# Stage 2's scores as products over 64 rows with two experts side by side, q and k kept unstacked, and three buffers of transposed probabilities

## The chip, the core and the metric

The program runs on one core of one Trainium2 chip. The metric is the device time of one execution in microseconds (us). TensorE multiplies, VectorE (DVE), ScalarE (ACT) and GpSimd (POOL) work on its operands and results, and SyncE (SP) issues the DMAs in one queue.

## The reference, cut to what matters

Eight batches of 576 rows pass through three stages. Stage 1 is an attention over 32 memory slots per head (8 heads of 64), the MLP mixes and applies a 512 to 2048 to 512 network, and stage 2 is a layer of four attention experts with 64 columns each, of which two are chosen for every row:

```python
# stage 1, per batch and head
a = softmax(phi)                       # over s, eps in the sum
k_m, v_m = a.T @ k, a.T @ v            # 32 x 64
attn = softmax(q @ k_m.T / 8) @ v_m
# mlp, per batch
u = x + (U @ V mixing over the sequence)
x = u + relu(u @ w_ch1) @ w_ch2
# stage 2, per batch
logits = x @ w_gate; top 2 of 4, weights w by softmax
for e in range(4):
    q, k, v = x @ wq[e], x @ wk[e], x @ wv[e]        # 576 x 64
    scores = q @ k.T / 8, causal
    ye = softmax(scores) @ v @ wo[e]
    out += (w of e where e was chosen) * ye
```

Every matrix product is made of three float16 products: both operands are split into a high and a low half, and high by high, high by low and low by high are added up in PSUM.

## The kernel before, in words

The batches are pipelined: in the loop over b (1 to 6) the MLP of batch b, stage 2 of batch b-1 and stage 1 of batch b+1 are put into one list of generator steps, ordered by a due time. One unit of due time is one item of the MLP, and a batch has 64 items of 12 matmuls each (`up`, L1000, and `down`, L1016). The last MLP and the last two stages 2 (called P and L in the list) follow `ORDER2`, a list written out by hand of which step comes when. A scheduler then sets each engine's order from the steps, their dependencies and the free buffers.

Stage 2 of a batch: `proj` (L1103) makes q and k of an expert pair `ep` (two experts, 2 x 64 lanes) for half the sequence, 288 columns. Its result is evicted into stacked tiles: `qst` holds for each expert the high half of q on lanes 0 to 63 and the low half on lanes 64 to 127; `khs` holds the high half of k twice, `kls` the low half twice. For q that takes two ACT copies (L1118) and two DVE subtractions (L1121) on 64 lanes, for k two ACT copies (L1125), two DVE subtractions (L1128), two more ACT copies (L1131) and one DVE copy (L1133).

`unit_s(i, ep, eo)` makes the scores of row block i (0 to 3) for one expert eo of the pair: two matmuls over 128 rows, (i+1)*128 columns wide (L1223, L1224), into one PSUM bank. Both split products of the high k and the low one are made at once by the stacking. Then come mask and maximum (DVE, L1227), exponential and high half (ACT, L1233, L1234), low half (POOL, L1236), and a transposing DMA into `pT` (SP, L1238), of which there are two buffers. `unit_s_last` does the last 64 rows of both experts in one go: eight matmuls of 64 weight columns and 288 columns (L1251, L1252), where one expert's result lies on PSUM lanes 0 to 63 and the other's on 64 to 127. `unit_v` (L1300) multiplies `pT` with v; its due time stands `A_LAG` = 4.2 units after that of its `unit_s`. `unit_o` and `unit_w` follow it.

In stage 1, `pair_scores` (L685 to L687) multiplies q with the memory keys: for each of six blocks of 96 rows three matmuls, whose weights have 96 columns, 64 columns wide.

PSUM has four banks called "a" that stage 1, `proj`, `vg`, the scores and small sums share, three "m" for the MLP, and one "v" for `unit_v`.

Of the kernel before, what the change touches and what calls it, by code (L numbers as in the profile page):

```python
# [20 lines left out]
P = 128  # L21
# [20 lines left out]
PRB, OBB = 1, 1  # L42


B_GAP, A_GAP, A_LAG = 10, 2.2, 4.2

START, SLACK, SLACK2, LATER = 53, 1.5, 4, 2

# [102 lines left out]
def kernel(ctx: ExitStack, tc: tile.TileContext, q, k, v, phi, U, V, w1, w2, wg, wq, wk, wv, wo, out):  # L151
# [27 lines left out]
    def ps_a(name):  # L179
        return ps.tile([P, 512], F32, tag="a", bufs=4, name=name)  # L180
# [326 lines left out]
    def stage1(b):  # L507
# [101 lines left out]
        def pair_scale(p):  # L609
            s = bpool.tile([P, 3], F32, tag="ps", bufs=4, name="ps")  # L610
            r = bpool.tile([P, 3], F32, tag="pi", bufs=2, name="pi")
            t = bpool.tile([P, 2], F32, tag="pt", bufs=6, name="pt")
            sb["s", p] = t
            sb["sc", p] = s
            yield from scales(largest(sb.pop(("arr", p))), s, r, down=2.0 ** -13)
            yield 0.1
            dve.scalar_tensor_tensor(t[:, 0:1], r[:, 2:3], 1.0 / 32.0, r[:, 0:1], op0=ALU.mult, op1=ALU.mult)
            dve.tensor_scalar(t[:, 1:2], r[:, 1:2], 1.0 / 64.0, None, op0=ALU.mult)
# [60 lines left out]
        def pair_scores(p):  # L679
            kb, vb = sb.pop(("kb", p))  # L680
            qT = sb.pop(("qT", p))
            psc = ps_a(f"ss{b}_{p}")
            for c in range(C):
                o = psc[:SP, c * 64:(c + 1) * 64]
                pe.matmul(o, qT[:, 0, c], kb[:, 0], start=True, stop=False)  # L685
                pe.matmul(o, qT[:, 0, c], kb[:, 1], start=False, stop=False)
                pe.matmul(o, qT[:, 1, c], kb[:, 0], start=False, stop=True)  # L687
            sb["psc", p] = psc
            pv = ps_a(f"vt{b}_{p}")
            pe.transpose(pv[:, 0:P], vb, ident)  # L690
            hf, pp = divmod(p, 2)
            if pp == 0:
                sb["vtf", hf] = bpool.tile([P, 2, P], F32, tag="vtf", bufs=1, name="vtf")
                sb["vth", hf] = bpool.tile([P, 2, 2, P], F16, tag="vth", bufs=2, name="vth")
            vtf, vth = sb["vtf", hf], sb["vth", hf]
            yield 0.4
            act.activation(vtf[:, pp], pv[:, 0:P], AF.Copy)
            act.activation(vth[:, pp, 0], pv[:, 0:P], AF.Copy)
            yield 0.4
            pool.tensor_tensor(vth[:, pp, 1], vtf[:, pp], vth[:, pp, 0], op=ALU.subtract)  # L700
# [13 lines left out]

        def half_kb_first(hf):
            pk = sb.pop(("pk", hf))
            iv = bpool.tile([P, 3], F32, tag="iv", bufs=2, name="iv")
            dve.tensor_scalar(iv[:, 2:3], pk[:, P:P + 1], EPS, None, op0=ALU.add)
            yield 0.1
            dve.reciprocal(iv[:, 2:3], iv[:, 2:3])  # L720
# [320 lines left out]
    def stage2(b):  # L1041
# [11 lines left out]
        def room(v, o, n):  # L1053
            return v[:, o:o + n]
# [40 lines left out]
        def proj(which, ep, h_):  # L1095
            yhl = s2["yhl"]
            w = (wqs, wks)[which]
            pp = ps_a(f"pj{b}_{which}_{ep}_{h_}")
            n = 0
            ts_ = slice(h_ * NH, (h_ + 1) * NH)  # L1100
            for kc in range(KC):
                for a, c in ((0, 0), (0, 1), (1, 0)):
                    pe.matmul(pp[:, 0:NH], w[:, a, kc, ep * P:(ep + 1) * P], yhl[:, c, kc, ts_],  # L1103
                              start=(n == 0), stop=(n == 3 * KC - 1))
                    n += 1
            yield 0.7
            if h_ == 0:
                for j, nm in enumerate((("qst",), ("khs", "kls"))[which]):
                    if tail:
                        o = 2 * KC * S + 2 * NT * NE * D + (3 * ep + which + j) * 2 * S  # L1110
                        s2[nm, ep] = room(v1, o, 2 * S).rearrange("p (e s) -> p e s", e=2)
                    else:
                        s2[nm, ep] = ap.tile([P, 2, S], F16, tag=nm, name=nm)
            src = [pp[eo * 64:eo * 64 + 64, 0:NH] for eo in range(2)]
            if which == 0:
                qst = s2["qst", ep]
                for eo in range(2):
                    act.activation(qst[0:64, eo, ts_], src[eo], AF.Copy)  # L1118
                yield
                for eo in range(2):  # L1120
                    dve.tensor_tensor(qst[64:128, eo, ts_], src[eo], qst[0:64, eo, ts_], op=ALU.subtract)  # L1121
            else:
                khs, kls = s2["khs", ep], s2["kls", ep]
                for eo in range(2):
                    act.activation(khs[0:64, eo, ts_], src[eo], AF.Copy)  # L1125
                yield
                for eo in range(2):
                    dve.tensor_tensor(kls[0:64, eo, ts_], src[eo], khs[0:64, eo, ts_], op=ALU.subtract)  # L1128
                yield
                for eo in range(2):  # L1130
                    act.activation(khs[64:128, eo, ts_], src[eo], AF.Copy)  # L1131
                yield
                dve.tensor_copy(kls[64:128, :, ts_], kls[0:64, :, ts_])  # L1133

        def vg(i):
            n = P if i < NT - 1 else TAIL
# [69 lines left out]
        def p_tiles(nb, k):  # L1206
            if tail:
                pr = ring(k, v2, 0, 2 * S, 3).bitcast(F32)
                phl = ring(k, v2, 6 * S, 2 * NT * P, 4)
                pT = ring(k, v2, 6 * S + 8 * NT * P, 2 * NT * P, 6)[:, 0:nb * P].rearrange("p (n q) -> p n q", q=P)  # L1210
                return pr, phl, pT
            pr = ap.tile([P, S], F32, tag="pr", bufs=PRB, name="pr")
            phl = ap.tile([P, 2 * NT * P], F16, tag="phl", bufs=2, name="phl")
            pT = ap.tile([P, nb, P], F16, tag="pT", bufs=2, name="pT")
            return pr, phl, pT

        def unit_s(i, ep, eo):
            qst, khs, kls = s2["qst", ep], s2["khs", ep], s2["kls", ep]
            cs = s2["ysc"][3]
            n = (i + 1) * P  # L1220
            nb = 2 * (i + 1)
            psc = ps_a(f"sc{b}_{i}_{ep}_{eo}")
            pe.matmul(psc[:, 0:n], qst[:, eo, i * P:n], khs[:, eo, 0:n], start=True, stop=False)  # L1223
            pe.matmul(psc[:, 0:n], qst[:, eo, i * P:n], kls[:, eo, 0:n], start=False, stop=True)  # L1224
            yield 0.5
            nm = ap.tile([P, 1], F32, tag="nm", bufs=4, name="nm")
            dve.tensor_tensor_reduce(psc[:, 0:n], psc[:, 0:n], wmask[:, (NT - 2 - i) * P:(NT - 1) * P], cs, 3.0e38, ALU.add, ALU.min, nm)  # L1227
# [12 lines left out]

        def unit_s_last(ep):
            i = NT - 1
            qst, khs, kls = s2["qst", ep], s2["khs", ep], s2["kls", ep]
            cs = s2["ysc"][3]
            psc = [ps_a(f"sc{b}_{i}_{ep}_{h_}") for h_ in range(2)]
            nb = 2 * NT
            N = NT * P
            for h_ in range(2):
                for eo in range(2):
                    o = psc[h_][eo * 64:eo * 64 + TAIL, 0:NH]  # L1250
                    pe.matmul(o, qst[:, eo, i * P:S], khs[:, eo, h_ * NH:(h_ + 1) * NH], start=True, stop=False)  # L1251
                    pe.matmul(o, qst[:, eo, i * P:S], kls[:, eo, h_ * NH:(h_ + 1) * NH], start=False, stop=True)  # L1252
            yield
            nm = ap.tile([P, 4], F32, tag="nml", bufs=2, name="nml")
            for h_ in range(2):
# [303 lines left out]
```

## Time and profile before

| | |
|---|---|
| median of 3 runs | 1362.08 us (1360.62 to 1370.35) |
| profiled execution, its own time | 1368.24 us |
| span of the profiled execution | 1366.3 us |
| PE busy | 1242.5 us (91%) |
| DVE busy | 938.0 us (69%) |
| ACT busy | 786.8 us (58%) |
| POOL busy | 409.2 us (30%) |

The profile lists for each engine its instructions with start and duration, and for each idle stretch what ended it. A matmul's duration runs from its start to the end of its result, while the next matmul starts long before; what a matmul costs an engine that is never idle is the distance from its start to the start of the next one. The timeline gives these starts; it merges like instructions that follow each other and gives their number.

### The profile page before, as it was taken

The numbers are of one execution on the slowest core, as the hardware profiler recorded it, in microseconds if no ns is written. First come the engines' busy times: TensorE is split into PE (matmuls) and PEld (weight loads), VectorE is DVE, ScalarE is ACT, GpSimd is POOL, SyncE is SP. The second block draws the span as 40 slices with busy tenths as digits, with TensorE's granted clock in tenths as the row PEclk, the third lists the DMA queues.
The fourth block names the chain that finished last, engine by engine and source line by source line (L and its number), as shares of the span: only waits on it lengthen the run. The fifth ranks groups of instructions, "written<-read, shape, count | busy, mean of one in ns | idle before, by whom it ended". The sixth has DMA issues, their size and how long they took to land. (4 is left out here: it accounts for less than half of the span.)

```text
span 1366.3 us, 31204 instructions
## 1 busy us (share of the span) xinstructions
PE 1242.5 (91%) x11932; PEld 950.9 (70%) x11932; DVE 938.0 (69%) x2791; ACT 786.8 (58%) x1886; POOL 409.2 (30%) x379
## 2 busy tenths in 40 slices
PE   5657897999999999999999999999999999999997
PEld 4435675777767777777777777677877777787764
DVE  7899777876577656876667766676667765554464
ACT  3885653665565654665655565565556566433476
POOL 3556620242322332332322323333222323001121
PEclk9778898999999999999999999999999999999999
DMA  9744141054412433244322434235232323102235
GB/s 253 229 141 123 36 89 27 21 97 73 89 48 61 92 75 60 58 83 89 74 60 61 85 59 87 58 74 98 57 69 63 75 57 63 49 14 41 39 77 113
DMA packets 257158, 106.42 MB, mean 78 GB/s; under 512 B 203792, under 2 KB 248528, under 8 KB 257008
## 3 DMA queue, kind: packets, MB, share of 16 engines
q1 hardware_dynamic: 257008, 104.43, 34.4%
q8 instruction: 93, 1.52, 0.5%
q14 instruction: 57, 0.47, 0.1%
HBM read 52.21 MB, written 9.44 MB: 45 GB/s over the span
## 5 line engine op out<-in xcount | busy, mean ns | idle before, releaser
L1000 PE MATMUL up<-uhl,w1s 128*128 128x288 f16 x3072 | 428.6, 293 | 27.2 <-DVE h L1006 22.5
L1016 PE MATMUL dn<-h,w2s 128*128 128x288 f16 x3072 | 411.8, 287 | 4.6 <-DVE u L1023 2.4
L1000 PEld LDWEIGHTS <-w1s 128*128 128x128 f16 x3072 | 301.3, 100 | 119.1 <-issue 34.9
L1016 PEld LDWEIGHTS <-w2s 128*128 128x128 f16 x3072 | 295.2, 98 | 84.4 <-issue 8.5
L1236 POOL TENSOR_TENSOR phl<-pr,phl 128x128 f16<-128x128 f32 (+3 forms) x112 | 92.5, 826 | 338.8 <-ACT phl L1234 253.1
L1006 DVE SCALAR_TENSOR_TENSOR h<-up,h 128x288 f16<-128x288 f32 x256 | 113.5, 451 | 60.5 <-ACT h L1004 59.3
L1004 ACT ACTIVATE h<-up 128x288 f16<-128x288 f32 x256 | 101.1, 402 | 85.3 <-PE up L1000 83.2
L605 DVE TENSOR_REDUCE amax<-raw 96x1 f32<-96x768 f32 x72 | 68.1, 946 | 87.2 <-DMA raw<-in_v_dram 46.5
L638 POOL TENSOR_TENSOR kvq<-raw,kvq 96x768 f16<-96x768 f32 x48 | 78.3, 1650 | 134.8 <-ACT raw L632 134.8
L1233 ACT ACTIVATE pr<-sc,nm 128x128 f32<-128x128 f32 (+3 forms) x112 | 58.8, 525 | 103.9 <-DVE nm L1227 54.1
L1023 DVE SCALAR_TENSOR_TENSOR u<-dn,us,u 128x288 f32<-128x288 f32 x128 | 65.2, 511 | 45.1 <-PE dn L1016 44.3
L1300 PEld LDWEIGHTS <-pT 128*128 128x128 f16 (+1 forms) x1260 | 56.5, 102 | 36.4 <-DMA pT<-phl 19.0
L1300 PE MATMUL av<-vhl,pT 128*128 128x64 f16 (+1 forms) x1260 | 68.7, 195 | 14.2 <-DMA pT<-phl 12.6
L1227 DVE CUSTOM_DVE_ANT_0 sc<-sc,wmask,ysc 128x128 f32<-128x128 f32 (+3 forms) x128 | 69.6, 549 | 9.3 <-PE sc L1224 8.1
L626 ACT ACTIVATE kvq<-raw,ps 96x768 f16<-96x768 f32 x72 | 63.0, 924 | 9.2 <-DVE ps L265 9.1
L1234 ACT ACTIVATE phl<-pr 128x128 f16<-128x128 f32 (+3 forms) x112 | 52.3, 467 | 15.3 <-DMA pT<-phl 13.2
L1337 ACT ACTIVATE ohl<-av,fac 128x64 f16<-128x64 f32 (+1 forms) x140 | 35.7, 307 | 41.9 <-DVE fac L1313 21.7
L1358 PE MATMUL wo<-wos,oT 128*128 128x512 f16 (+1 forms) x288 | 57.5, 351 | 2.5 <-DMA oT<-ohl 1.3
L1103 PE MATMUL pj<-yhl,wqs 128*128 128x288 f16 x336 | 47.6, 290 | 5.6 <-ACT u L885 4.9
L1103 PEld LDWEIGHTS <-wqs 128*128 128x128 f16 x384 | 38.0, 101 | 17.8 <-issue 6.8
L1151 PE MATMUL vg<-wvg,yhl 128*128 128x260 f16 (+1 forms) x504 | 48.5, 256 | 0.0
L1103 PE MATMUL pj<-yhl,wks 128*128 128x288 f16 x336 | 46.3, 286 | 0.0
(323 smaller groups left out, 2264.7 us busy)
## 6 DMA issues: line engine op xcount, KB each, us to landing
w1s<-in_moe_w_ch_dram SPq DMA_DIRECT2D x32, 256.0 KB, 5.1
w2r<-in_moe_w_ch_dram SPq DMA_DIRECT2D x8, 1024.0 KB, 5.1
out_dram<-ob SPq DMA_DIRECT2D x28, 256.0 KB, 2.2
raw<-in_k_dram SPq DMA_DIRECT2D x48, 144.0 KB, 2.6
raw<-in_v_dram SPq DMA_DIRECT2D x48, 144.0 KB, 2.9
raw<-in_q_dram SPq DMA_DIRECT2D x48, 144.0 KB, 2.5
phi<-in_phi_dram SPq DMA_DIRECT2D x16, 288.0 KB, 3.8
rx<-in_k_dram SPq DMA_DIRECT2D x16, 144.0 KB, 4.6
```

The lines of the kernel that those rows point to most:

```text
L605: dve.tensor_reduce(o, raw, axis=AX.XYZ, op=ALU.max, apply_absolute_value=True)
L626: act.activation(hl[:, 0], src, AF.Copy, scale=s[0:SP, j:j + 1])
L638: pool.tensor_tensor(hl[:, 1], src, hl[:, 0], op=ALU.subtract)
L1000: pe.matmul(pm, w1s[:, f // 2, a, kc, f % 2 * P:f % 2 * P + P], uhl[c][:, kc], start=(n == 0), stop=(n == 3 * KC - 1))
L1004: act.activation(hb[:, 0, g], pm, AF.Relu)
L1006: dve.scalar_tensor_tensor(hb[:, 1, g], pm, 0.0, hb[:, 0, g], op0=ALU.max, op1=ALU.subtract)
L1016: pe.matmul(pm, w2s[:, m, fg, a, g], hb[:, c, g], start=(g == 0 and a + c == 0), stop=(g == FG - 1 and a == 1))
L1023: dve.scalar_tensor_tensor(y, pm, st["us", b][:, 4 + KC * fg + m:5 + KC * fg + m], y, op0=ALU.mult, op1=ALU.add)
L1103: pe.matmul(pp[:, 0:NH], w[:, a, kc, ep * P:(ep + 1) * P], yhl[:, c, kc, ts_], start=(n == 0), stop=(n == 3 * KC - 1))
L1227: dve.tensor_tensor_reduce(psc[:, 0:n], psc[:, 0:n], wmask[:, (NT - 2 - i) * P:(NT - 1) * P], cs, 3.0e38, ALU.add, ALU.min, nm)
L1236: (dve if tail and TD >> (2*i + eo) & 1 else pool).tensor_tensor(phl[:, n:2 * n], pr[:, 0:n], phl[:, 0:n], op=ALU.subtract)
L1300: pe.matmul(pav[:n, eo * D:(eo + 1) * D], lhs, vhl[:kn, c, j, vs], start=(j == 0 and a + c == 0), stop=(j == i and a == 1))
```

## The change

The q and k of an expert pair are kept as they come from `proj`, both experts on 128 lanes, in four tiles: qh, ql, kh, kl. A product of scores now runs over the 64 rows of one expert, and the three split products are three matmuls. `products` issues them for both experts in turn (rows 0 to 63, rows 64 to 127), into two banks. In `unit_s` the first of the two experts of a block that is called takes both banks and issues all six matmuls; the other finds its bank filled. `pair_scores` takes 128 weight columns in five of its six blocks; the surplus 32 result lanes are not read. `A_LAG` and the buffers of `pT`, `pt` and `iv` change. `ORDER2` stays as it is; `proj` of k has three steps in place of five.

```diff
-B_GAP, A_GAP, A_LAG = 10, 2.2, 4.2
+B_GAP, A_GAP, A_LAG = 10, 2.2, 6.3
...
-            t = bpool.tile([P, 2], F32, tag="pt", bufs=6, name="pt")
+            t = bpool.tile([P, 2], F32, tag="pt", bufs=5, name="pt")
...
+            qf = qT.rearrange("p a c t -> p (a c t)")
             for c in range(C):
-                o = psc[:SP, c * 64:(c + 1) * 64]
-                pe.matmul(o, qT[:, 0, c], kb[:, 0], start=True, stop=False)
-                pe.matmul(o, qT[:, 0, c], kb[:, 1], start=False, stop=False)
-                pe.matmul(o, qT[:, 1, c], kb[:, 0], start=False, stop=True)
+                for n, (x, y) in enumerate(((0, 0), (0, 1), (1, 0))):
+                    t = (x * C + c) * SP
+                    w = P if c < C - 1 else SP
+                    pe.matmul(psc[:w, c * 64:(c + 1) * 64], qf[:, t:t + w], kb[:, y], start=(n == 0), stop=(n == 2))
...
-            iv = bpool.tile([P, 3], F32, tag="iv", bufs=2, name="iv")
+            iv = bpool.tile([P, 3], F32, tag="iv", bufs=1, name="iv")
...
-            if h_ == 0:
-                for j, nm in enumerate((("qst",), ("khs", "kls"))[which]):
+            for x, nm in enumerate((("qh", "ql"), ("kh", "kl"))[which]):
+                if h_ == 0:
                     if tail:
-                        o = 2 * KC * S + 2 * NT * NE * D + (3 * ep + which + j) * 2 * S
-                        s2[nm, ep] = room(v1, o, 2 * S).rearrange("p (e s) -> p e s", e=2)
+                        o = 2 * KC * S + 2 * NT * NE * D + (4 * ep + 2 * which + x) * S
+                        s2[nm, ep] = room(v1, o, S)
                     else:
-                        s2[nm, ep] = ap.tile([P, 2, S], F16, tag=nm, name=nm)
-            src = [pp[eo * 64:eo * 64 + 64, 0:NH] for eo in range(2)]
-            if which == 0:
-                qst = s2["qst", ep]
-                for eo in range(2):
-                    act.activation(qst[0:64, eo, ts_], src[eo], AF.Copy)
-                yield
-                for eo in range(2):
-                    dve.tensor_tensor(qst[64:128, eo, ts_], src[eo], qst[0:64, eo, ts_], op=ALU.subtract)
-            else:
-                khs, kls = s2["khs", ep], s2["kls", ep]
-                for eo in range(2):
-                    act.activation(khs[0:64, eo, ts_], src[eo], AF.Copy)
-                yield
-                for eo in range(2):
-                    dve.tensor_tensor(kls[0:64, eo, ts_], src[eo], khs[0:64, eo, ts_], op=ALU.subtract)
-                yield
-                for eo in range(2):
-                    act.activation(khs[64:128, eo, ts_], src[eo], AF.Copy)
-                yield
-                dve.tensor_copy(kls[64:128, :, ts_], kls[0:64, :, ts_])
+                        s2[nm, ep] = ap.tile([P, S], F16, tag=nm, name=nm)
+                d = s2[nm, ep][:, ts_]
+                if x == 0:
+                    act.activation(d, pp[:, 0:NH], AF.Copy)
+                    hi = d
+                    yield
+                else:
+                    dve.tensor_tensor(d, pp[:, 0:NH], hi, op=ALU.subtract)
...
-            pT = ap.tile([P, nb, P], F16, tag="pT", bufs=2, name="pT")
+            pT = ap.tile([P, nb, P], F16, tag="pT", bufs=3, name="pT")
...
+        def products(ep, qs, outs):
+            for n_, (x, y) in enumerate((("qh", "kh"), ("qh", "kl"), ("ql", "kh"))):
+                for eo in range(2):
+                    r = slice(64 * eo, 64 * eo + 64)
+                    o, ks = outs(eo)
+                    pe.matmul(o, s2[x, ep][r, qs], s2[y, ep][r, ks], start=(n_ == 0), stop=(n_ == 2))
...
-            psc = ps_a(f"sc{b}_{i}_{ep}_{eo}")
-            pe.matmul(psc[:, 0:n], qst[:, eo, i * P:n], khs[:, eo, 0:n], start=True, stop=False)
-            pe.matmul(psc[:, 0:n], qst[:, eo, i * P:n], kls[:, eo, 0:n], start=False, stop=True)
+            if ("psc", i, ep) not in s2:
+                two = [ps_a(f"sc{b}_{i}_{ep}_{x}") for x in range(2)]
+                products(ep, slice(i * P, n), lambda x: (two[x][:, 0:n], slice(0, n)))
+                s2["psc", i, ep] = two
+            psc = s2["psc", i, ep][eo]
...
-            for h_ in range(2):
-                for eo in range(2):
-                    o = psc[h_][eo * 64:eo * 64 + TAIL, 0:NH]
-                    pe.matmul(o, qst[:, eo, i * P:S], khs[:, eo, h_ * NH:(h_ + 1) * NH], start=True, stop=False)
-                    pe.matmul(o, qst[:, eo, i * P:S], kls[:, eo, h_ * NH:(h_ + 1) * NH], start=False, stop=True)
+            for z in range(2):
+                products(ep, slice(i * P, S), lambda x: (psc[x ^ z][x * 64:x * 64 + TAIL, 0:NH],
+                                                            slice((x ^ z) * NH, (x ^ z) * NH + NH)))
```

## Rows read from the trace of the kernel before

**Rows 1.** Busy time by stretch: start:end, us; PE, PEld, DVE, ACT, POOL busy (instructions); clock, DMA

```profile
500.00:800.00 300.00, 282.23 (x2816) 218.62 (x2814) 204.58 (x642) 174.77 (x435) 91.55 (x86) 1.00 0.36 74
1100.00:1230.00 130.00, 128.28 (x1218) 99.87 (x1217) 74.19 (x234) 70.59 (x188) 22.80 (x25) 1.00 0.20 44
1320.00:1350.00 30.00, 27.00 (x309) 18.92 (x307) 23.50 (x96) 27.52 (x89) 12.04 (x16) 1.00 0.46 102
```

**Rows 2.** PE's waits, 300 to 1230 us: waiting line, releaser: us, times, longest

```profile
PE up L1000 <- DVE h L1006: 18.3, 13, 2.8
PE av L1300 <- DMA pT<-phl: 12.0, 18, 1.5
PE pj L1103 <- ACT u L885: 4.9, 3, 1.6
```

**Rows 3.** Waits of SP's queue, whole span: waiting line, releaser: us, times, longest

```profile
SPq L1238 <- PE av L1300: 44.1, 24, 8.4
```

**Rows 4.** Costliest ACT and DVE groups by shape: xcount | busy us, mean ns | idle before

```profile
L1118 ACT ACTIVATE qst<-pj 64x288 f16<-64x288 f32 x56 | 22.6, 403 | 36.1 <-PE pj L1103 35.7
L1004 ACT ACTIVATE h<-up 128x288 f16<-128x288 f32 x256 | 101.1, 402 | 85.3 <-PE up L1000 83.2
...
L1121 DVE TENSOR_TENSOR qst<-pj,qst 64x288 f16<-64x288 f32 x56 | 25.5, 456 | 9.2 <-ACT qst L1118 8.2
L1006 DVE SCALAR_TENSOR_TENSOR h<-up,h 128x288 f16<-128x288 f32 x256 | 113.5, 451 | 60.5 <-ACT h L1004 59.3
L1133 DVE COPY kls<-kls 64x576 f16<-64x576 f16 x28 | 10.1, 359 | 0.9
```

**Rows 5.** PE's timeline around two `unit_s`: start us, us, line, shape, number

```profile
361.92 0.38 PE L1223 MATMUL sc<-khs,qst 128*128 128x512 f16 x1
362.14 0.38 PE L1224 MATMUL sc<-kls,qst 128*128 128x512 f16 x1
362.35 0.53 PE L1000 MATMUL up<-uhl,w1s 128*128 128x288 f16 x3
...
1337.57 0.22 PE L1223 MATMUL sc<-w1s 128*128 128x128 f16 x1
1337.62 0.22 PE L1224 MATMUL sc<-w1s 128*128 128x128 f16 x1
1337.68 0.51 PE L1300 MATMUL av<-w1s,w2s 128*128 128x64 f16 x12
1338.03 0.27 PE L1223 MATMUL sc<-w1s 128*128 128x256 f16 x1
1338.14 0.27 PE L1224 MATMUL sc<-w1s 128*128 128x256 f16 x1
```

**Rows 6.** PE's timeline around a `unit_s_last`

```profile
1301.77 1.46 PE L1358 MATMUL wo<-wos,oT 128*128 128x512 f16 x6
1303.16 0.32 PE L1251 MATMUL sc<-khs,qst 128*64 128x288 f16 x2
1303.31 0.29 PE L1252 MATMUL sc<-kls,qst 128*64 128x288 f16 x2
1303.43 0.29 PE L1251 MATMUL sc<-khs,qst 128*64 128x288 f16 x2
...
1303.78 0.43 PE L1300 MATMUL av<-vhl,pT 128*128 128x64 f16 x9
```

**Rows 7.** PE's timeline around a transposition over 64 rows

```profile
1348.39 0.38 PE L1358 MATMUL wo<-wos,oT 128*128 128x512 f16 x1
1348.70 0.27 PE L1328 MATMUL oT<-ident,o 64*128 64x64 f32 x1
1348.91 0.82 PE L1358 MATMUL wo<-wos,oT 128*128 128x512 f16 x3
```

**Rows 8.** PE's timeline of a `pair_scores`, first and last of 17 matmuls

```profile
772.10 0.21 PE L686 MATMUL ss<-kb,qT 128*96 128x64 f16 x1
...
772.82 0.21 PE L687 MATMUL ss<-kb,qT 128*96 128x64 f16 x1
```

More of the change, by code (lines that the diff above doesn't have):

```diff
@@ L1213, in p_tiles @@
             phl = ap.tile([P, 2 * NT * P], F16, tag="phl", bufs=2, name="phl")
-            pT = ap.tile([P, nb, P], F16, tag="pT", bufs=2, name="pT")
+            pT = ap.tile([P, nb, P], F16, tag="pT", bufs=3, name="pT")
             return pr, phl, pT
+        def products(ep, qs, outs):
[4 more added lines that the diff above has]
+                    pe.matmul(o, s2[x, ep][r, qs], s2[y, ep][r, ks], start=(n_ == 0), stop=(n_ == 2))
         def unit_s(i, ep, eo):
-            qst, khs, kls = s2["qst", ep], s2["khs", ep], s2["kls", ep]
             cs = s2["ysc"][3]
@@ L1242, in unit_s_last @@
             i = NT - 1
-            qst, khs, kls = s2["qst", ep], s2["khs", ep], s2["kls", ep]
             cs = s2["ysc"][3]
```

## The prediction

> **What bounds the kernel now.** I read the busy time by stretch first: there the reader is to see that PE works nearly all the time between the start-up and the last 50 us (282.2 of 300 us, then 128.3 of 130) at a granted clock of 1.00, the 2.4 GHz level, while DVE stands at 68% and ACT at 58% of the same 300 us [rows 1]. Only the last part is different: from 1320 to 1350 us ACT is busy for 27.5 of 30 us and PE for 27.0. So up to 1320 us the time is the sum of PE's matmuls, start to start, and of PE's waits; work of ACT or DVE counts only where PE waits for it. PE's waits came second: between 300 and 1230 us the long ones are `up` waiting for DVE to empty a PSUM bank (18.3 us in 13 waits), `unit_v` waiting for the transposed probabilities (12.0 us in 18 waits, 1.5 us the longest) and `proj` waiting for a bank "a" that ACT holds (4.9 us in three) [rows 2]. Third came PE's timeline, for the distance between starts, since the durations overlap [rows 5 to 8].
>
> **The change part by part.** Counts come from the code: 8 batches, 2 expert pairs each, 4 blocks i.
>
> *Scores of `unit_s`.* A 512-column product takes 0.215 us from start to start (361.92 to 362.35 in two), one of 256 columns 0.11, one of 128 columns 0.055 [rows 5]; 384 lies between, 0.16. The four widths make 0.54 us. Before, a block costs four products (two experts, two each). Afterwards there are six, over 64 rows. If the two experts run side by side, that is the time of three, and each of the 16 (batch, pair) gains 0.54 us: -8.6 us. If they don't, it is the time of six, 1.08 us lost instead: +17.3 us. The trace of before shows no two products on different rows at once. What it shows is two on different columns: in `unit_s_last` eight matmuls of 288 columns take four slots of 0.12 us, two in each (1303.31, 1303.43) [rows 6]. I take side by side, that nearest row. The Trainium skill (TensorE: Matmul & The Clock Gate, Part 3, packing small matmuls) says that products on distinct row groups run together and gives 3.07 times for four of them; no run here shows it yet. By that figure a second product would add about a tenth to a slot (4/3.07 less 1, over three), an estimate from that page, and the sum below would be 2.6 us higher.
>
> *The switch of shape.* Before, `unit_s` used the whole array, like its neighbours. Now each block is an excursion to half the rows. What an excursion costs is seen at `unit_s_last`: six products of 512 columns ahead of it take 1.39 us to the next start, where 6 x 0.215 is 1.29, so 0.10 on the way in; its four slots take 0.62 us instead of 4 x 0.12, so 0.14 inside and on the way out [rows 6]. Together 0.24 us. That this holds for rows too is seen at a transposition over 64 rows: the 512-column product ahead of it takes 0.31 us instead of 0.215 [rows 7]. 64 blocks x 0.24 us = +15.4 us; the lower bound is 0. With this, the scores of `unit_s` cost 6.8 us more than before, although their products cost less.
>
> *Scores of `unit_s_last`.* It is such an excursion already. Eight matmuls in four slots become twelve in six, on opposite corners of the array: 16 x 2 x 0.12 = +3.8 us. Not side by side they are twelve slots: +15.4 us.
>
> *`pair_scores`.* Its 96-column weights are paced at 0.045 us (17 matmuls, 16 distances, 772.10 to 772.82) [rows 8]; matmuls of the same width with 128 columns of weights follow each other at 0.029 us (twelve from 1337.68 to 1338.03) [rows 5]. 7 batches x 4 pairs x 15 of 18 matmuls = 420, by 0.016 us: -6.7 us, on PE's path.
>
> *Eviction of `proj`.* An operation on 128 lanes costs what one on 64 does: ACT 402 against 403 ns, DVE 451 against 456 [rows 4]. For q two and two become one and one; for k four ACT and three DVE operations become one and one. Over 64 calls (half of them k) 128 ACT operations of 0.403 us go (51.6 us), and 96 of DVE (64 of 0.456, 32 of 0.359: 40.7 us). Beside a PE that is never idle this is worth nothing of itself; the matmuls of `up` and `down` cover it. It is on the path in the last part, where ACT is busy 92% [rows 1]: batch L has 8 calls and loses 16 x 0.403 = 6.4 us of ACT. I take half, -3 us, since only the calls of one expert pair of two fall into that stretch; bounds 0 and -6.4. A second place where it could count is the 18.3 us of `up` behind DVE; in front of those waits stand mostly splits and maxima that the change leaves alone, so I take 0 there and keep -9, half, as the bound.
>
> *Three `pT`, `A_LAG` 6.3.* SP's queue waits 44.1 us at the transposing DMA until `unit_v` has given a buffer back (24 times, 8.4 us the longest), and everything behind it in the queue, the loads of stage 1 among it, waits too [rows 3]. The transposed tile then comes late for PE, 12.0 us [rows 2]. A unit of due time is twelve matmuls, at least 12 x 0.12 = 1.4 us, so `unit_v` comes at least 3 us later, twice the longest of its waits. I take the whole: -12 us; bound 0. `unit_o` and `unit_w` move with it; they are due after the batch's 64 units either way and other MLP work fills PE. Fewer `pt` and `iv` cost nothing: at most three `pt` are alive, and the two uses of `iv` lie 11 units apart.
>
> *PSUM.* The second expert's bank is now taken about 2.2 units earlier. In the loop that leaves the four banks "a" enough by the due times. In `ORDER2` I counted the banks step by step: more than four are asked for at 3 places before and at 8 after, four of the new ones in P and L with little else for PE. A wait for such a bank lasted 1.6 us (4.9 in three) [rows 2]. I take two more of them, +3 us; 0 and 8 are the bounds inside the forecast.
>
> Sum: -8.6 + 15.4 + 3.8 - 6.7 - 3 - 12 + 3 = -8.1 us. The profiled execution took 1368.2 us, and 1360.1 by this; it stands 6 us above the median, so against the runs shown it is 1362.1 - 8.1 = 1354.0 us.
>
> **The rivals.** About 1%, 13.6 us, is what a measurement of this kernel can tell from no change.
>
> (A) The experts don't run side by side. Against it: columns do [rows 6]; for it: no row shows rows doing it. `unit_s` then costs 25.9 us more than in the forecast (16 x 3 x 0.54) and `unit_s_last` 11.5 (six slots more): -8.1 + 37.4 = +29.3, 1391 us, slower. It decides the sign from 8.1 us of the 37.4 on, when about a fifth of the products fail to overlap, and makes 1% from 8.1 + 13.6 = 21.7 us on, three fifths.
>
> (B) Splitting the rows alone costs no switch, as the weights stay 128 columns wide: -15.4 us more, 1338.6 us. Against it stands one transposition [rows 7]. The Trainium skill (TensorEngine Tiling (Array Packing), Key Properties) says that changing the tiling mode drains TensorE; by that rule (B) falls, and the trace's 0.10 us on the way in agrees.
>
> (C) The relief of DVE and of SP's queue reaches `up` after all: half of 18.3 us, 1345 us. For it: 68% busy DVE and a queue that blocks loads [rows 1, 3].
>
> (D) PSUM's four banks become the bound: a wait of 1.6 us at all 8 places and one in each of six batches is 22.4 us in place of 3, +11.3, 1373 us. For it: `proj` waits there already [rows 2].
>
> (E) The buffers don't do what they are for: `unit_v` waits as before, because POOL and ACT deliver late, not because a buffer lacks: +12, 1366 us.
>
> **How the numbers follow.** Forecast 0.36 (own range 1346 to 1362), A 0.15, B 0.14, C 0.16, D 0.09, E 0.10. Faster by over 1%, below 1348.5 us: all of B, most of C and the lower end of the forecast, 0.35. Slower, above 1375.7: A and a third of D, 0.18. Within 1%: 0.47. The range from 1336 to 1386 leaves out A and the outer ends of B and D.
>
> **What would show it.** Right: in a `unit_s`, pairs of matmuls of one start, three slots of 0.215 us at 512 columns, 0.10 us before and over 0.1 after; `pair_scores` at 0.029 us; PE's wait for `pT` near 0, and SP's wait for `unit_v` too; ACT some 50 and DVE some 40 us less busy. Wrong: six slots in a row (A), no gap at the switch (B), `up`'s waits for DVE halved (C), PE waiting in front of `products`, `proj` or `vg` for banks (D), `unit_v` still waiting (E). The prediction as a whole fails if PE is idle more than before at other places than these.

## The result and the profile after

| | before | after |
|---|---|---|
| median of all runs on one chip | 1362.64 us (1360.20 to 1370.35, 6 runs) | 1351.93 us (1348.17 to 1354.40, 6 runs) |
| ratio to before | | 0.9914, 95% interval 0.9889 to 0.9938 |
| profiled execution, its own time (span) | 1368.24 us (1366.3) | 1349.91 us (1347.8) |
| mean granted clock of TensorE | 0.969 | 0.980 |

The changed kernel is faster by 10.7 us of median, 0.9%, with an interval from 0.6 to 1.1%. The two profiled executions differ by 18.3 us, because before's stands 5.6 us above its median and after's 2.0 us below its own. Every account from the two traces has therefore 18 us to explain, and sizes under about 5 us are read from it with care.

The page of after, busy time of each engine over the whole span, then its two groups of the new eviction (operation, shape, count | busy us, mean ns | idle before):

```profile
PE 1243.9 (92%) x12124; PEld 935.5 (69%) x12124; DVE 897.5 (67%) x2695; ACT 731.0 (54%) x1758; POOL 413.7 (31%) x379
...
L1119 ACT ACTIVATE qh<-pj 128x288 f16<-128x288 f32 x28 | 11.4, 406 | 29.5 <-PE pj L1105 29.4
L1123 DVE TENSOR_TENSOR kl<-pj,kh 128x288 f16<-128x288 f32 x28 | 12.6, 449 | 8.0 <-ACT kh L1119 8.0
```

ACT is busy 55.8 us less and DVE 40.5 us less than before; the prediction said 50 and 40. PE is busy for as long as before, in a span that is 18.5 us shorter: what was lost is idle time. (That PE is busy for no longer although it does more has to do with its clock, which the last section weighs.)

The busy time by stretch of after (the last stretch lies 18 us earlier than before's, as the end does; columns as in [rows 1]):

```profile
500.00:800.00 300.00, 292.21 (x2938) 222.19 (x2935) 202.88 (x640) 166.61 (x417) 94.92 (x86) 1.00 0.33 71
1100.00:1230.00 130.00, 130.00 (x1207) 97.98 (x1205) 64.50 (x210) 58.24 (x157) 21.36 (x26) 1.00 0.20 39
1302.00:1332.00 30.00, 28.42 (x324) 18.83 (x322) 18.85 (x83) 20.80 (x68) 9.35 (x12) 1.00 0.41 93
```

In the loop PE is idle for 7.8 of 300 us where it was for 17.8, and in the last MLP for nothing of 130 us [rows 1]. At the end ACT comes down from 27.5 to 20.8 of 30 us.

PE's waits of after between 300 and 1230 us, and SP's over the whole span (waiting line, releaser: us, times, longest):

```profile
PE up L1002 <- DVE h L1008: 9.9, 9, 1.7
PE wo L1356 <- DMA oT<-ohl: 5.3, 3, 2.2
PE ss L689 <- DVE kb L674: 3.9, 5, 1.2
...
SPq L1238 <- PE av L1298: 24.8, 10, 9.1
```

The wait of `unit_v` for the transposed probabilities, 12.0 us in 18 times [rows 2], has no line left; that of `proj` for ACT (4.9 us) has none either; that of `up` for DVE is down from 18.3 to 9.9 us, which the sum had not taken. SP's wait for `unit_v` has fallen from 44.1 us [rows 3] only to 24.8, where near 0 was foretold.

**The scores.** PE's timeline of after around a block of 256 columns (start us, us, line, shape, number):

```profile
641.43 0.28 PE L1214 MATMUL sc<-kh,qh 64*128 64x256 f16 x2
641.54 0.27 PE L1214 MATMUL sc<-kl,qh 64*128 64x256 f16 x2
641.65 0.27 PE L1214 MATMUL sc<-kh,ql 64*128 64x256 f16 x2
```

Two experts share each slot (x2), their starts 3 to 4 ns apart, and the slots follow at 0.11 us, the pace of one such product in [rows 5]: the rows run side by side. The next matmul starts at 641.86, 0.10 us later than a slot would end, so the way out costs what the way in was seen to cost [rows 6]. The Trainium skill (TensorE: Matmul & The Clock Gate, Part 3: packing small matmuls) says that products on distinct row groups start about 4 ns after one another; this trace agrees, with 3 to 4 ns.

A block of 512 columns in the same view looks otherwise:

```profile
351.49 0.39 PE L1214 MATMUL sc<-kh,qh 64*128 64x512 f16 x1
351.72 0.38 PE L1214 MATMUL sc<-kl,qh 64*128 64x512 f16 x1
351.93 0.38 PE L1214 MATMUL sc<-kh,ql 64*128 64x512 f16 x1
352.24 0.91 PE L1002 MATMUL up<-uhl,w1s 128*128 128x288 f16 x6
353.08 0.39 PE L1214 MATMUL sc<-kh,qh 64*128 64x512 f16 x1
353.31 0.38 PE L1214 MATMUL sc<-kl,qh 64*128 64x512 f16 x1
353.53 0.38 PE L1214 MATMUL sc<-kh,ql 64*128 64x512 f16 x1
353.83 0.30 PE L1002 MATMUL up<-uhl,w1s 128*128 128x288 f16 x1
```

Here the first expert's three products run alone, matmuls of `up` fill PE, and 1.6 us after the first come the second's three, alone too. Each expert's products need a bank of PSUM of their own, and the scheduler put other work on PE between the two. 14 of the 16 blocks of 512 columns are split, ten of them three and three as here, and others with them: the 64 blocks of `unit_s` stand in 96 runs of scores on PE, 96 excursions to half the rows in place of 64, and those that were split three and three gain nothing from the second half of the array.

Added up from start to start over the whole trace, the way in of each run counted with it, the scores of `unit_s` take 37.8 us before and 55.7 after, +17.9 where +6.8 was foretold; those of `unit_s_last` 12.1 and 16.0, +3.9 as foretold (+3.8); `pair_scores` 24.1 and 18.1, -6.0 (foretold -6.7).

From the end of each batch's last `down` the gain can be dated: after stands 0 us ahead of before at the end of batch 0's MLP, 6.2 after batch 1's, 14.3 after batch 2's, 15.0, 18.4, 16.5, 16.3 and 15.9 after the rest, and 18.5 at the end. It is made in the loop, in the batches where PE's waits went; the part behind the last MLP adds 2.6 us, all edits together.

### The profile page after: what moved, and what is told of

It reads as the page before. It is cut to its first block, busy times and chain, and to the rows that moved or that the text cites. A ratio compares the mean times of both kernels' runs of the same rounds, so it can differ in the third digit from the quotient of the medians.

```text
span 1347.8 us, 31258 instructions
## 1 busy us (share of the span) xinstructions
PE 1243.9 (92%) x12124; PEld 935.5 (69%) x12124; DVE 897.5 (67%) x2695; ACT 731.0 (54%) x1758; POOL 413.7 (31%) x379
## 5 line engine op out<-in xcount | busy, mean ns | idle before, releaser
L1002 PE MATMUL up<-uhl,w1s 128*128 128x288 f16 x3072 | 422.4, 290 | 17.6 <-DVE h L1008 13.6
L1002 PEld LDWEIGHTS <-w1s 128*128 128x128 f16 x3072 | 294.8, 99 | 113.6 <-issue 36.8
L1298 PEld LDWEIGHTS <-pT 128*128 128x128 f16 (+1 forms) x1260 | 59.9, 103 | 22.3 <-issue 12.1
L1227 DVE CUSTOM_DVE_ANT_0 sc<-sc,wmask,ysc 128x128 f32<-128x128 f32 (+3 forms) x128 | 67.0, 551 | 10.7 <-PE sc L1214 10.2
L1298 PE MATMUL av<-vhl,pT 128*128 128x64 f16 (+1 forms) x1260 | 71.9, 195 | 1.7 <-DVE ohl L1338 1.2
L1273 POOL TENSOR_TENSOR phl<-pr,phl 128x576 f16<-128x576 f32 x14 | 17.9, 1278 | 96.8 <-ACT phl L1263 96.6
```

The costliest lines, as they stand in the source:

```text
L1002: pe.matmul(pm, w1s[:, f // 2, a, kc, f % 2 * P:f % 2 * P + P], uhl[c][:, kc], start=(n == 0), stop=(n == 3 * KC - 1))
L1298: pe.matmul(pav[:n, eo * D:(eo + 1) * D], lhs, vhl[:kn, c, j, vs], start=(j == 0 and a + c == 0), stop=(j == i and a == 1))
```

## The experiments

The account so far has three places that the prediction did not see so: more excursions than blocks, a relief of `up`, and a wait of SP that stayed. Two readings were set against each other throughout. By the first PE's slots set the time, so that each microsecond saved or added on PE is one of the time, and the terms of the sum can be undone one by one. By the second the deliveries to PE (of `h` by DVE, of the transposed probabilities) set the time in the loop, and slots saved on PE come back as waits. All ratios are to the kernel before on the same chip, over five rounds; after is 0.9914, and 1 us is 0.00073. As the runs of one kernel scatter by some 5 us, an experiment's difference to after, which goes through the kernel before, is known to 4 or 5 us.

### Pairs by force

To see what the pairs are worth, a section that the scheduler may not interleave was put round the six products of a block (`crit`). On this base one expert's three products were put ahead of the other's, `pair_scores` was set back to 96 columns, and the old number of evictions came back.

```diff
-                products(ep, slice(i * P, n), lambda x: (two[x][:, 0:n], slice(0, n)))
+                with tc.tile_critical():
+                    products(ep, slice(i * P, n), lambda x: (two[x][:, 0:n], slice(0, n)))
```

> The changed kernel with the six products of each unit_s held together as one section that the scheduler may not split; nothing else differs. In the trace of the changed kernel the scores of unit_s stand in 96 separate runs on PE instead of 64, most 512-column blocks as three plus three, and cost 46.9 us of starts plus 8.8 us on the way in, 55.7 us; with every block whole they should cost 16 x 1.62 + 64 x 0.24 = 41 us. Theory 1 (the second bank comes late, so the scheduler splits the pair, and the products are on the path): 14 us less than the changed kernel, about 1338 us, a ratio of 0.982 to the kernel before. Theory 2 (the bank is the limit: PE then stands waiting for it instead): 1348 to 1356 us, PE idle in front of the products by up to 14 us.

Measured: 1428.47 us, ratio 1.0448 (1.0413 to 1.0484), 73 us slower than after. The waits of `crit` over the whole span say why (columns as above; PEld is the load of weights, which runs ahead of PE):

```profile
DVE sc L1228 <- PEq L1222: 100.1, 58, 5.5
PEld sc L1214 <- issue: 74.9, 69, 4.0
```

The load of weights in front of the products stands, for no producer that the profile shows, 74.9 us in 69 times (there are 64 sections). PE itself stands 58.0 us in front of the scores, where it stands 1.1 us in after, and all its waits add up to 161.1 us against 98.4. That is most of what is lost; it is the price of the section, and covers what the pairs may bring, though every block now stands on PE in one piece. The base is of no use for the question, and the three kernels built on it say less than they should.

`crit_serial`, one expert's products first, then the other's:

```diff
-            for n_, (x, y) in enumerate((("qh", "kh"), ("qh", "kl"), ("ql", "kh"))):
-                for eo in range(2):
+            if isinstance(qs, slice) and qs.stop < S:
+                order_ = [(n_, eo) for eo in range(2) for n_ in range(3)]
...
+            for n_, eo in order_:
...
```

> As crit, but in each unit_s the three products of one expert come first and then the three of the other, so that only the last of the first and the first of the second can run side by side: five slots instead of three. Theory 1 (running side by side is what the products gain): 16 x 2 x 0.54 = 17 us more than crit. Theory 2 (PE's products are not the path, or the pairing gives nothing): within 3 us of crit.

Measured: 1431.55 us, 1.0466 (1.0434 to 1.0499), 3 us above `crit`. Its timeline shows that the edit did not make the five slots that it was to make:

```profile
294.66 0.40 PE L1219 MATMUL sc<-kh,qh 64*128 64x512 f16 x2 [0.45 <-issue]
294.89 0.39 PE L1219 MATMUL sc<-kl,qh 64*128 64x512 f16 x2
295.11 0.39 PE L1219 MATMUL sc<-kh,ql 64*128 64x512 f16 x2
```

Although the program now names one expert's three products first, the two experts still share three slots, their starts 10 ns apart where `crit` has 3 to 4, in 58 of the 62 blocks that stand by themselves. Whether the scheduler or TensorE brings them together is not shown. So this run does not take the pairs apart and is inconclusive on what they are worth; it does show that the order of a block's six products in the program does not decide whether they pair.

`crit_ss96`, with `w = SP` in `pair_scores` (the diff stands below with `ss96`):

> As crit, with 96 columns of weights in all six blocks of pair_scores as before the change. Theory 1 (the 0.045 against 0.029 us of a matmul there are on PE's path): 6 to 7 us more than crit. Theory 2 (they lie beside other waits): within 3 us of crit.

Measured: 1426.66 us, 1.0434 (1.0398 to 1.0471), 2 us below `crit`: inconclusive, as the difference is within the error and PE stands in front of each block anyway.

`crit_evict`, with the old number of evictions, in one burst on each engine:

```diff
-                    act.activation(d, pp[:, 0:NH], AF.Copy)
+                    for eo in range(2 + 2 * which):
+                        r = slice(64 * (eo % 2), 64 * (eo % 2) + 64)
+                        act.activation(d[r], pp[r, 0:NH], AF.Copy)
...
-                    dve.tensor_tensor(d, pp[:, 0:NH], hi, op=ALU.subtract)
+                    for eo in range(2 + which):
+                        r = slice(64 * (eo % 2), 64 * (eo % 2) + 64)
+                        dve.tensor_tensor(d[r], pp[r, 0:NH], hi[r], op=ALU.subtract)
```

> As crit, but proj writes its results as often as before the change: two ACT and two DVE operations on 64 lanes for q, four ACT and three DVE for k, into the same tiles (values unchanged). ACT gets about 52 us and DVE about 40 us of work back. Forecast's theory (the relief counts only at the end): 3 us more than crit, PE's waits of up for DVE unchanged. Rival (C) (the relief is what shortened up's waits from 18.3 to 9.9 us): 8 to 12 us more than crit, and up's waits back near 18 us.

Measured: 1466.11 us, 1.0716 (1.0680 to 1.0752), 37 us above `crit`, the one clear answer of the four: the evictions are not free.

### The buffers and the lag

```diff
-B_GAP, A_GAP, A_LAG = 10, 2.2, 6.3
+B_GAP, A_GAP, A_LAG = 10, 2.2, 4.2
...
-            pT = ap.tile([P, nb, P], F16, tag="pT", bufs=3, name="pT")
+            pT = ap.tile([P, nb, P], F16, tag="pT", bufs=2, name="pT")
```

Both together are `lag_buf`, the lag alone `lag42`, the buffer alone `buf2`; `lag74` goes on to 7.4 with three buffers.

> The changed kernel with A_LAG 4.2 and two buffers of pT, as before the change; scores, eviction and pair_scores stay as changed. Forecast's theory (the third buffer and the later unit_v take away unit_v's waits for pT): 12 us more than the changed kernel, ratio 1.000 to the kernel before, and PE's wait of L1300's counterpart for the DMA back near 12 us between 300 and 1230 us. Rival (the waits went because eviction is lighter, so the transposes are fed earlier): 0 to 3 us more, the wait still near 0.

> The changed kernel with A_LAG 4.2, three buffers of pT kept. If the later unit_v is what took the waits for pT away: 10 to 13 us more than the changed kernel, ratio 0.999 to 1.001, unit_v's waits near 20 us. If the third buffer did it: within 3 us of the changed kernel, ratio 0.991.

> The changed kernel with two buffers of pT, A_LAG 6.3 kept. If the third buffer is what took the waits away: 10 to 13 us more than the changed kernel, ratio 0.999 to 1.001, and SP's queue waiting 60 us or more for unit_v, since a buffer is now held 2.1 units longer. If the later unit_v did it alone: within 3 us of the changed kernel, ratio 0.991.

> The changed kernel with A_LAG 7.4. In PE's order the scores stand in 88 runs instead of 96 and cost 5 us less at the prices of the trace. If PE's products are what counts: 1346 to 1349 us, ratio 0.988. If waits take their place, as in the run that held the second products back: 1352 to 1358 us, ratio 0.991 to 0.996.

Measured: `lag_buf` 1367.47 us, 1.0011 (0.9987 to 1.0036), 13 us above after; `lag42` 1365.73 us, 1.0002 (0.9975 to 1.0028), 12 us above; `buf2` 1353.38 us, 0.9907 (0.9882 to 0.9932), the same as after; `lag74` 1366.35 us, 0.9998 (0.9980 to 1.0016), 11.5 us above. PE's waits from 300 to 1230 us, first of `lag42`, with two lines of it:

```profile
PE av L1298 <- DMA pT<-phl: 14.7, 12, 3.1
PE up L1002 <- DVE h L1008: 13.6, 12, 2.1
```

then of `buf2`, and behind them its SP queue over the whole span:

```profile
PE up L1002 <- DVE h L1008: 10.2, 9, 1.7
PE wo L1356 <- DMA oT<-ohl: 4.3, 3, 1.5
...
SPq L1238 <- PE av L1298: 115.6, 41, 9.4
```

With the old lag `unit_v` waits for the transposition again, 14.7 us, although it has three buffers; with two buffers and the new lag it does not wait, although SP's queue stands 115.6 us for a buffer, 2.6 times as long as before [rows 3]. The lag took the wait away. The third buffer is worth nothing here, and SP's wait does no harm. A third buffer in the kernel before was not tried.

`lag74` has no wait for the transposition either, but `up` waits for DVE 23.3 us in the same stretch, the longest 3.9 us:

```profile
PE up L1002 <- DVE h L1008: 23.3, 11, 3.9
PE av L1298 <- DVE ohl L1338: 5.8, 6, 1.6
```

A later `unit_v` is therefore not simply safer: 1.1 units more lose what 2.1 had gained. In the four waits of 3.9 us DVE does six splits of stage 2's input in a row (`yhl`, 3.75 us) and a reduction of stage 1 (1.0 us) directly ahead of the `h` that `up` waits for; why the scheduler's order turns out so is open. At those waits and the one of 2.7 us lie five dips of the granted clock to 0.50, 24 us in all, which may have cost up to 12 us; the last section says more of such dips.

### The evictions

`evict` puts the edit of `crit_evict` into the kernel after, without the section. `evict_steps` brings the old number back in the old steps, the further ones for k in steps of their own:

```diff
+                half = [slice(64 * eo, 64 * eo + 64) for eo in range(2)]
...
-                    act.activation(d, pp[:, 0:NH], AF.Copy)
+                    for r in half:
+                        act.activation(d[r], pp[r, 0:NH], AF.Copy)
...
-                    dve.tensor_tensor(d, pp[:, 0:NH], hi, op=ALU.subtract)
+                    for r in half:
+                        dve.tensor_tensor(d[r], pp[r, 0:NH], hi[r], op=ALU.subtract)
+                    if which:
+                        yield
+                        for r in half:
+                            act.activation(hi[r], pp[r, 0:NH], AF.Copy)
+                        yield
+                        dve.tensor_tensor(d[half[0]], pp[half[0], 0:NH], hi[half[0]], op=ALU.subtract)
```

> The changed kernel, but proj writes its results as often as before the change (two ACT and two DVE operations on 64 lanes for q, four and three for k; values unchanged): 52 us of ACT and 40 us of DVE come back. In the order in which PE's products now stand, nine more runs of scores are apart, worth 4 us at the prices of the trace. Forecast's theory (relief counts only in the last part, 3 us): 7 us more than the changed kernel, up's waits for DVE stay near 10 us. Rival (C) (the relief shortened up's waits): 13 to 16 us more, up's waits back near 18 us.

> The changed kernel with the number of eviction operations as before the change, as in evict, but in the steps in which they stood before (for k two ACT, two DVE, two ACT, one DVE, other work between), not in bursts. Values unchanged. PE's order of the scores costs 5 us more than in the changed kernel at the prices of the trace. Theory 1 (the relief itself is worth much: evict's 39 us come from 52 us of ACT and 40 us of DVE in queues that PE waits for): 29 to 39 us more than the changed kernel, ratio 1.013 to 1.020, unit_v's and up's waits back near 17 and 19 us. Theory 2 (evict was slow because its operations came in bursts of four and three): 5 to 12 us more, ratio 0.995 to 1.000.

Measured: `evict` 1393.96 us, 1.0199 (1.0168 to 1.0230), 39 us above after; `evict_steps` 1375.93 us, 1.0081 (1.0053 to 1.0108), 22.7 us above. The burst is harsher than what before did, as it holds the bank and both queues at one go, so `evict_steps` is the fair price. PE's waits in it from 300 to 1230 us:

```profile
PE up L1002 <- DVE h L1008: 22.5, 13, 2.5
PE av L1307 <- DMA pT<-phl: 3.0, 5, 1.6
```

`up` waits for DVE 22.5 us again, where after has 9.9. From start to start its scores take 5.8 us more than after's, since more blocks are split; the other 17 us or so are what the relief of ACT and DVE was worth, but not as waits of PE alone. At the end of the last MLP `evict_steps` stands 14.9 us behind after and at the end 22.8, so 8 us arise in the last part. Of the 14.9 us the scores are 5. PE's waits up to there, all added up, are only 1.3 us longer than in after, as others became shorter while `up`'s grew. What is left fits the clock: up to there, from 298 us on, it falls to 0.50 five times for 3.4 us each, four times at a wait of `up` of 2.0 to 2.5 us, where after has no such dip. One of them, in columns as in [rows 1]:

```profile
558.10:561.40 3.30, 3.30 (x14) 2.14 (x13) 3.06 (x10) 0.91 (x2) 2.31 (x2) 0.50 0.05 10
```

The five are at most 8.5 us at half speed, an upper bound. What stands directly ahead of `h` on DVE in the long waits is, as in before, mostly the split of a value into its halves or a maximum, and not an eviction of `proj`: that the relief acts by moving the whole queue forward is argued from this and was not tried.

### The pairs kept together, and pair_scores

`hold` asks the scheduler to issue the later products of a block only behind the second expert's first product, without a section:

```diff
+            second = None
...
-                    pe.matmul(o, s2[x, ep][r, qs], s2[y, ep][r, ks], start=(n_ == 0), stop=(n_ == 2))
+                    with tc.issue_after(second) if second is not None else nullcontext():
+                        pe.matmul(o, s2[x, ep][r, qs], s2[y, ep][r, ks], start=(n_ == 0), stop=(n_ == 2))
+                    if n_ == 0 and eo == 1:
+                        second = nc.cur_bb.bb.instructions[-1]
```

> The changed kernel, with the second and third product of either expert queued behind the first product of the second expert, so that a bank that comes late splits a block as one and five instead of three and three; no section, no wait is added. In PE's order 14 blocks of 512 columns lose two of their six slots; at the prices of the trace the scores fall from 59.5 to 52.3 us (unit_s) and from 18.1 to 16.3 us (unit_s_last). Theory 1 (banks come late, the scheduler splits the pairs, the lost slots are on PE's path): 9 us less than the changed kernel, about 1343 us, ratio 0.985. Theory 2 (the late bank is the path: holding one expert's products back delays its softmax): 0 to 5 us more than the changed kernel, and PE waits in front of unit_v.

Measured: 1357.60 us, 0.9941 (0.9918 to 0.9965), 4 us above after, where the first reading wanted 9 less. From 300 us on the scores take 52.3 us in place of 57.5, without the way in, so the slots are saved; PE's waits, which add up to 38.1 us there in place of 30.7, take more than that back:

```profile
PE up L1002 <- DVE h L1008: 15.8, 13, 2.4
PE es L578 <- POOL es L576: 3.1, 3, 1.0
```

`ss96` sets `pair_scores` back to 96 columns in the kernel after:

```diff
-                    w = P if c < C - 1 else SP
+                    w = SP
```

> The changed kernel with 96 weight columns in all blocks of pair_scores, as before the change. Forecast's theory (0.016 us on PE's path in each of 420 matmuls): 6 to 7 us more than the changed kernel, ratio 0.996. Rival (these matmuls lie where PE would wait anyway): within 2 us of the changed kernel, ratio 0.991.

Measured: 1355.11 us, 0.9921 (0.9897 to 0.9946), 1 us above after, give or take 5. The 6 or 7 us were not seen. The trace has them on PE: `pair_scores` takes 24.5 us instead of 18.1 from start to start, while PE's waits from 300 us on, added up, are 26.6 us instead of 30.7.

### What the experiments share

The page has one row for `up`, with PE's idle time in front of it over the whole span (behind the second bar) and what ended most of it. After, `buf2`, `hold`, `evict_steps` and `lag74`, in this order, one fence each:

```profile
L1002 PE MATMUL up<-uhl,w1s 128*128 128x288 f16 x3072 | 422.4, 290 | 17.6 <-DVE h L1008 13.6
```

```profile
L1002 PE MATMUL up<-uhl,w1s 128*128 128x288 f16 x3072 | 426.4, 292 | 17.9 <-DVE h L1008 13.5
```

```profile
L1002 PE MATMUL up<-uhl,w1s 128*128 128x288 f16 x3072 | 427.0, 292 | 25.8 <-DVE h L1008 22.0
```

```profile
L1002 PE MATMUL up<-uhl,w1s 128*128 128x288 f16 x3072 | 427.0, 292 | 30.5 <-DVE h L1008 26.7
```

```profile
L1002 PE MATMUL up<-uhl,w1s 128*128 128x288 f16 x3072 | 431.1, 294 | 33.1 <-DVE h L1008 29.3
```

The two quicker kernels have 18 us here, the two slower ones 30 and more (1375.93 and 1366.35 us), `hold` lies between. So `up` behind DVE is one place where an edit elsewhere in the loop is paid out: the slots that `hold` saved (5.2 us) came back as 8.2 us in this row. It is not the only one: `evict`, the slowest of the kernels without a section, has 25.8 us here, as `hold` does, and `lag42` 24.8; their `unit_v` waits too. The second reading holds for small savings on PE, and the first only for the sum of slots, waits and what the clock adds.

## Why the prediction came out right

The time, 1351.93 us, lies 2 us from the predicted 1354.0, and faster by 0.9% is within the 1% that was called likeliest. That the sum came so close is luck in part: two of its steps were far out, in opposite directions.

| term of the sum | predicted | shown |
|---|---|---|
| scores of `unit_s`, products and switches | +6.8 | +17.9 on PE, from start to start |
| scores of `unit_s_last` | +3.8 | +3.9 on PE |
| `pair_scores` | -6.7 | -6.0 on PE; +1 ± 5 of the time when undone |
| eviction, at the end | -3 | about -7 (`evict_steps` behind the last MLP, its dearer scores deducted) |
| eviction, in the loop (rival C) | 0 | about -10 (`evict_steps` to the end of the last MLP, its dearer scores deducted), up to 8.5 of it by the clock |
| lag and third buffer | -12 | -12 by the lag, 0 by the buffer |
| PSUM, as waits of PE | +3 | no such wait left; blocks are split instead |
| sum, against the medians | -8.1 | -10.7 |

The rows of the right column come from different kinds of measurement, from slots of PE and from whole kernels, and need not add up to the last line; the table says which terms were mis-sized.

**Side by side** was right, and (A) wrong: three slots a pair, as [rows 6] had shown for columns. **The price of an excursion** was nearly right, 0.10 us out beside 0.10 in where 0.24 was taken for both, and (B) wrong. The Trainium skill (TensorEngine Tiling (Array Packing), Key Properties) says that a change of the tiling mode drains TensorE, and this trace agrees, with 0.10 us at each end.

**The number of excursions** is the mis-sized step: it took "64 blocks x 0.24 us", one excursion each with both experts in it. The runs showed 96, and the 512-column blocks, which were to bring 0.215 of the 0.54 us a pair gains, mostly one expert at a time: 11 us more than foretold. The cause that I would name is that of rival D, a second bank that is asked for early and comes late; that it is the bank and not another claim of the scheduler is argued and was not tried. In any case PE did not wait, as D had it; other work filled the time and the pair was split.

**The eviction** was mis-sized the other way, by "I take 0 there", where the runs show about 10 us, and by "I take half, -3 us", where they show about 7, at its bound of -6.4. For the 0, two rows had been weighed: 68% busy DVE, and splits and maxima standing ahead of the long waits. That a queue is a third idle on average, and that the work to be removed does not stand directly in front of a wait, were no evidence that removing it leaves the wait alone. It was rival C, given 0.16, and its price of -9 is about what the loop shows. `up`'s waits did fall by half, as C had it, and came back in `evict_steps`; but in sum PE's waits in the loop hardly differ between after and `evict_steps` (1.3 us), and the larger part of the price is the clock, which neither C nor the forecast had.

**The lag** was right in size for what the prediction put in one term, 12 us (12 and 13 measured), and in one half of its mechanism, the later `unit_v`. The other half, its account of SP's queue, was wrong: that the buffers' wait [rows 3] made the transposed tile late. The wait grew to 115.6 us in `buf2` and cost nothing. What had been late was `unit_v`'s due time, which came too early for a chain of mask, exponential, low half and transposition.

**`pair_scores`** was right on PE and is not seen in the time. It had been booked as "on PE's path"; in the loop PE's path is partly waits for DVE, and those take up most of what is saved (`ss96`: 6.4 us more on PE, 4.1 us less of waits).

Open: what the pairs themselves bring, since no kernel could force them without other costs, and none took them apart; what the scores cost in time, since no run puts the old scores into the kernel after, so that +17.9 and +3.9 stand on PE's slots alone; why a lag of 7.4 orders DVE's work as it does; and how much of the 17 us of the eviction is fewer operations and how much fewer steps, as `evict_steps` brings back both.

## What to carry to other kernels

Before a saving on the busiest engine is booked as time, ask which wait of that engine will swallow it; and before relief of a half-idle engine is booked as nothing, look at whether the busiest engine ever waits for it. Two results that are to be computed side by side need both their banks at once, and a scheduler may put them one after the other, with other work between, without any wait to show for it: count runs of matmuls in the timeline, not waits. Here a late operand was cured by the due time of its reader and not by another buffer, and a queue's long wait is no cost until some engine is shown to wait for what stands behind it.

## What was not expected of the hardware

The clock takes part in the difference of the two traces. Before, PE's stretches around 312 us (us, then PE, PEld, DVE, ACT, POOL busy, granted clock, DMA share, GB/s):

```profile
310.00:311.60 1.60, 0.19 (x2) 0.00 (x0) 0.81 (x1) 0.56 (x4) 1.29 (x2) 1.00 0.39 85
...
313.40:315.20 1.80, 1.80 (x10) 1.07 (x8) 1.00 (x3) 0.66 (x3) 0.00 (x0) 0.50 0.19 35
```

PE stood for 1.43 us, waiting for the transposed probabilities until 311.6 us; then the granted clock fell to 0.50, the 1.2 GHz level, while PE was busy all the time; this dip lasted 3.4 us. Before has six such dips from 300 us on (at 312, 482, 1032, 1080, 1309 and 1353 us), after none until its end. Each of the six comes right behind a wait of PE of 1.4 to 2.8 us; but 20 other waits of over 1 us in before brought none, nor did the 12 of after, up to 2.2 us. Six times 3.4 us at half speed are at most 10 us, an upper bound, of the 18 by which the two traces differ. A wait of PE can so cost more than its own length: at 312 us, up to 1.7 us on top of 1.4. The prediction priced waits at their length alone.

This also closes the account of the two traces. The scores and `pair_scores` put 15.8 us more on PE, and PE's waits over the whole span fell from 118.4 to 98.4 us; that alone would be 4 us. The mean granted clock rose from 0.969 to 0.980: the lower level can have cost at most 3.1% of 1366 us before, 42 us, and 2.0% of 1348 us after, 27 us. These 15 us, an upper bound again, are about what is missing of the 18.
